# Key-value sums with the exponentiated keys stationary, and key projections in 128-column matmuls

## The chip, the cores and the metric

The kernel runs on one core of a Trainium2 chip. The metric is the device time of one execution in microseconds (us). TensorE (PE in the profile) multiplies matrices: a weight load (PEld) brings the stationary operand into the array, then a matmul streams the moving operand past it and writes to a bank of PSUM. VectorE (DVE), ScalarE (ACT) and GpSimd (POOL) do the rest; SyncE (SP) issues transfers.

## The reference

Linear attention with exponential features, then a feed-forward layer on its output:

```python
def phi(x):
    proj = np.einsum('bhsd,df->bhsf', x, w_phi)
    proj = proj - np.max(np.abs(proj), axis=-1, keepdims=True)
    return np.concatenate([np.exp(proj), np.exp(-proj)], axis=-1)
q_p, k_p = (phi(q), phi(k))
kv = np.einsum('bhsf,bhsd->bhfd', k_p, v)
z = np.sum(k_p, axis=2)
num = np.einsum('bhsf,bhfd->bhsd', q_p, kv)
den = np.einsum('bhsf,bhf->bhs', q_p, z)[..., None] + 1e-06
...
h = x @ w_in
g = np.maximum(0.01 * h, h)
return (g @ w_out).astype(np.float32)
```

There are 8 batches, 8 heads, 576 tokens, head size 64, 128 projected features (256 after the two exponentials); x has 4608 rows of 512, the hidden layer 2048. All is float32.

## The kernel before

**Precision.** A float32 matmul takes several passes, so most operands are split: a value rounded to the type F32R (names ending in h) and the remainder, again F32R (ending in l). A product is then the sum of three F32R matmuls, h with h, l with h and h with l, accumulated in one PSUM bank.

**Feed-forward.** 18 blocks of 256 tokens, each with 16 feature tiles. `layer1` (L549) issues 12 matmuls of 256 columns into a tile `h`; ScalarE and VectorE apply the leaky maximum (L559, L560), ScalarE rounds it to `gh`, POOL makes `gl`; `layer2` (L565), three tiles later, issues six matmuls of 512 columns into `acc`. Before a block, `split` (L537) rounds its rows of attention output (`xh`, `xl`).

**Attention.** A phase handles two heads of one batch: `k_phase(i)` and `q_phase(i)`, i from 0 to 31. The first four are written apart, for the start. Phases 4 to 7 of `k_phase` (`nat`) use float32 matmuls for the sums; phases 8 to 31, 24 of them, split. In such a phase each of the five 128-token chunks (the last has 64 tokens) is projected by two matmuls with the keys stationary (`ks`, in whose 128 rows rounded key and remainder of one head lie together) and 256 moving columns, `wq`, rounded weights beside their remainders (L231). The two halves of the result are added by ScalarE and VectorE (L235, L236). Then come the maximum (L239), the subtraction (L244) and two exponentials (L249, L250). Rounding gives `kph` and `kpl`. The sums then have the values stationary, `vh` (64 rounded values and two columns of ones) or `vl` (64 remainders), and 256 feature columns of keys moving, six matmuls for a chunk. For the last chunk rounded keys and remainders are stacked in 128 rows (`kst`), and `vl` multiplies 64 of them. All accumulate in one tile `c`, with features along the columns. ScalarE copies it (L275), four transposes turn it (L281), and it is rounded and split into `kvh` and `kvl` (L291 to L294), which `q_phase` uses as stationary operands (L358 to L363).

**Order.** The code emits instructions with priorities (attention ahead of the feed-forward layers), and a scheduler writes one fixed order for each engine. `advance` (L586) lets attention run ahead, up to two phases and the room in `ring`. Tiles are drawn from pools: `PBUFS` (L34) gives the eight PSUM banks to tags: three for `a` (projections and numerators), one for `c`, two for `h`, two for `acc`. A tile waits until the last reader of its buffer is done.

Of the kernel before, what the change touches and what calls it, by code (L numbers as in the profile page):

```python
# [9 lines left out]
F32 = mybir.dt.float32  # L10
F32R = mybir.dt.float32r
# [3 lines left out]
ALU = mybir.AluOpType  # L15
AX = mybir.AxisListType

P = 128
B, H, S, D = 8, 8, 576, 64
NP = H // 2  # L20
F = 128
# [8 lines left out]
LAG = 3  # L30
NN = 8
NK = 8
BUFS = {"kph": 2, "eq": 2, "m4": 2, "g": 2, "gh": 2, "gl": 2, "qh": 2, "ql": 2}
PBUFS = {"a": 3, "c": 1, "h": 2, "acc": 2}  # L34
ENG = {"vh": "a", "kst": "v", "qh": "v", "o": "av", "kl": "pv", "kpl": "pppv", "ksub": "vvp"}
TINY = 2.0 ** -15
HUGE = 2.0 ** 16 * 1.875
# [7 lines left out]
def attention_moe_kernel(ctx: ExitStack, tc: tile.TileContext, q, k, v, vt, w_phi, w_in, w_out, out):  # L45
    nc = tc.nc
# [16 lines left out]

    def copy_(key, o, i):
        e = pick(key) or "a"
        if e == "a":
            nc.scalar.copy(o, i)  # L67
        else:
            (nc.vector if e == "v" else nc.gpsimd).tensor_copy(o, i)  # L69

    def tt_(key, o, a, b, op):
        (nc.vector if pick(key) == "v" else nc.gpsimd).tensor_tensor(o, a, b, op=op)  # L72
# [23 lines left out]
    vh = ct([P, 10, 66], F32R, "vh")  # L96
    vl = ct([P, 10, 64], F32R, "vl")
    nc.gpsimd.memset(vh[:, :, 64:66].bitcast(F32), 1.0)
# [41 lines left out]
    for j in range(2):  # L140
        r = slice(64 * j, 64 * j + 64)
        c = slice(F * j, F * j + F)
# [46 lines left out]
    def k_phase(i):  # L189
        nat = i < NK  # L190
        rk, rv = kraw.pop(i)
        ks = st([P, 2, S], F32R, "ks")
        kh, kl = ks[:, 0], ks[:, 1]
        if nat:
            copy_("kh", kh, rk)
            tt_("kl", kl, rk, kh.bitcast(F32), ALU.subtract)
        else:
            for j in range(2):
                o, n = slice(64 * j, 64 * j + 64), slice(64 - 64 * j, 128 - 64 * j)
                copy_("kh", ks[o, j], rk[o])  # L200
                nc.vector.tensor_tensor(ks[n, j], rk[o], ks[o, j].bitcast(F32), op=ALU.subtract)
            copy_("vh", vh[:, :, 0:64], rv[:, :, 0:64])
            for r, c in ((slice(0, P), slice(0, 8)), (slice(64, P), slice(8, 10))):
                tt_("vl", vl[r, c], rv[r, c, 0:64], vh[r, c, 0:64].bitcast(F32), ALU.subtract)
        if i + 1 < B * NP:
            load_k(i + 1)
        yield
        kvp = pt("c")

        def kv_mm(j, lt, rt, first=False, last=False):  # L210
            nc.tensor.matmul(kvp[0 : lt.shape[1], 256 * j : 256 * j + 256], lhsT=lt, rhs=rt,  # L211
                             start=first and j == 0, stop=last, skip_group_check=True)

        for g in range(3):
            w = 2 if g < 2 else 1
            r = slice(0, P) if g < 2 else slice(64, P)
            n = P if g < 2 else 64
            m4 = st([P, 4], F32, "m4")
            pmk = st([P, 4, F], F32, "pmk")
            if nat:  # L220
                pk = pt("a")
                for s in range(w):
                    t0 = (2 * g + s) * P if g < 2 else S - P
                    proj(pk, s, kh[:, t0 : t0 + P], kl[:, t0 : t0 + P])
                pkv = pk[r, 0 : 256 * w].rearrange("p (a f) -> p a f", f=F)
            else:
                for s in range(w):
                    t0 = (2 * g + s) * P if g < 2 else S - P
                    pk = pt("a")
                    for j in range(2):  # L230
                        nc.tensor.matmul(pk[:, 256 * j : 256 * j + 256], lhsT=ks[:, j, t0 : t0 + P],  # L231
                                         rhs=wq.rearrange("p a f -> p (a f)"), start=True, stop=True)
                    pk = pk[r].rearrange("p (j x f) -> p j x f", j=2, x=2)
                    x = pmk[r, 2 * s : 2 * s + 2]
                    copy_("pk", x, pk[:, :, 1])  # L235
                    nc.vector.tensor_tensor(x, pk[:, :, 0], x, op=ALU.add)  # L236
                    yield
                pkv = pmk[r, 0 : 2 * w]
            nc.vector.tensor_reduce(m4[r, 0 : 2 * w], pkv, axis=AX.X, op=ALU.max, apply_absolute_value=True)  # L239
            mb = m4[r, 0 : 2 * w].unsqueeze(2).broadcast_to([n, 2 * w, F])  # L240
            if nat:
                nc.vector.tensor_tensor(pmk[r, 0 : 2 * w], pkv, mb, op=ALU.subtract)
            else:
                tt_("ksub", pkv, pkv, mb, ALU.subtract)  # L244
            yield
            for s in range(w):
                c = 2 * g + s
                ek = st([P, 2, 256], F32, ("ek", "kph", "kpl")[c % 3] if nat else "ek")
                nc.scalar.activation(ek[r, :, 0:F], pmk[r, 2 * s : 2 * s + 2], AF.Exp)  # L249
                nc.scalar.activation(ek[r, :, F:256], pmk[r, 2 * s : 2 * s + 2], AF.Exp, scale=-1.0)  # L250
                if nat:
                    for j in range(2):
                        kv_mm(j, rv[r, 4 * j + c if c < 4 else 8 + j], ek[r, j], first=c == 0, last=c == 4)
# [20 lines left out]
        kvs = st([P, 2, 256], F32, "ek").rearrange("p a (b f) -> p a b f", b=2)[0:66]  # L274
        copy_("kvs", kvs, kvp[0:66].rearrange("p (a b f) -> p a b f", a=2, b=2))  # L275
        yield
        kvt = pt("c")
        kvtv = kvt[:, 0:264].rearrange("p (a b f) -> p a b f", a=2, b=2)
        for j in range(2):
            for t in range(2):  # L280
                nc.tensor.transpose(kvtv[:, j, t], kvs[:, j, t], ident[0:66, 0:66])  # L281
        if i < NN:
            kvh = st([P, 2, 2, P], F32, "kvh")
            nc.scalar.copy(kvh[:, :, :, 0:64], kvtv[:, :, :, 0:64])
            nc.scalar.copy(kvh[:, :, :, 64:P], kvtv[:, :, :, 64:65].broadcast_to([P, 2, 2, 64]))
            kvs_of[i] = kvh, None
        else:
            kvh = st([P, 2, 2, P], F32R, "kvh")
            kvl = st([P, 2, 2, P], F32R, "kvl")
            zb = kvtv[:, :, :, 64:65].broadcast_to([P, 2, 2, 64])  # L290
            copy_("kvh", kvh[:, :, :, 0:64], kvtv[:, :, :, 0:64])  # L291
            copy_("kvh", kvh[:, :, :, 64:P], zb)
            nc.vector.tensor_tensor(kvl[:, :, :, 0:64], kvtv[:, :, :, 0:64], kvh[:, :, :, 0:64].bitcast(F32), op=ALU.subtract)
            nc.vector.tensor_tensor(kvl[:, :, :, 64:P], zb, kvh[:, :, :, 64:P].bitcast(F32), op=ALU.subtract)  # L294
            kvs_of[i] = kvh, kvl
        yield

# [362 lines left out]
```

## Time and profile before

| | |
|---|---|
| runs (three) | 1284.26, 1285.53, 1285.65 us; median 1285.53 |
| profiled execution | span 1285.0 us from first to last instruction; its time outside the span is not given |
| TensorE busy, matmuls | 1199.9 us, 7564, each with a weight load |
| VectorE, ScalarE, GpSimd busy | 972.6, 775.9, 778.4 us |
| TensorE clock granted | 0.973 on average, 1.00 from 300 to 1110 us |

A row of the timeline gives start and length in us, engine, line, operation, tiles written and read, and shapes; `x4` at its end merges four equal neighbours, and brackets show idle time before it and what ended it. A row of the groups gives the count, total busy us and mean ns of one, then the idle time before and its releasers. The length of a matmul row includes its latency; matmuls overlap, so their pace is read from start to start. In shapes, `128*66` is rows and columns of the stationary operand, `128x256` the moving one; the type reads f32 for F32R operands too.

### The profile page before, as it was taken

The page shows a single profiled execution, that of the slowest core. Times are in us where ns is not written, and L with a number is a line of the kernel's source. Part 1 is how long each engine was busy: PE and PEld are TensorE (multiplying, and loading weights), DVE is VectorE, ACT ScalarE, POOL GpSimd, SP SyncE. Part 2 cuts the span into 40 slices and gives each one's busy share as a digit, 9 for nine tenths or more (in the row PEclk, how much of TensorE's full clock was granted, in tenths as well). Part 3 has the DMA queues.
Part 4 walks back from the last instruction along what each step waited for, and adds up shares of the span by engine and source line. Part 5 has one row for each costly group of instructions (what it writes and reads, how often), then busy time and mean ns, then how long its engine had stood idle before and what let it go on. Part 6 is the DMA issues. An engine that isn't in the chain of part 4 may idle for free. (4 is left out here: it accounts for less than half of the span.)

```text
span 1285.0 us, 21831 instructions
## 1 busy us (share of the span) xinstructions
PE 1199.9 (93%) x7564; PEld 1045.4 (81%) x7564; DVE 972.6 (76%) x1685; ACT 775.9 (60%) x2014; POOL 778.4 (61%) x784
## 2 busy tenths in 40 slices
PE   7778879989999999999999999999999999999998
PEld 5457648868888888879888888989888988899997
DVE  7999996578898988888988998872888798611111
ACT  5454447666666776766767766753767766533232
POOL 3677754255676777676867677764677766533232
PEclk9789879999999999999999999999999999999999
DMA  7333341111110111111111111110111110000000
GB/s 202 113 88 97 118 121 46 40 35 29 30 43 24 46 30 46 30 37 38 29 46 30 45 30 37 30 36 11 36 30 46 30 37 1 17 18 1 18 17 17
DMA packets 62782, 57.05 MB, mean 44 GB/s; under 512 B 45136, under 2 KB 46288, under 8 KB 62672
## 3 DMA queue, kind: packets, MB, share of 16 engines
q1 hardware_dynamic: 62672, 55.65, 15.3%
q8 instruction: 60, 0.98, 0.3%
q14 instruction: 50, 0.41, 0.1%
HBM read 46.20 MB, written 9.44 MB: 43 GB/s over the span
## 5 line engine op out<-in xcount | busy, mean ns | idle before, releaser
L72 POOL TENSOR_TENSOR gl<-g,gh 128x256 fp32r<-128x256 f32 x288 | 241.5, 842 | 252.9 <-ACT gh L67 212.3
L552 PE MATMUL h<-xh,w0h 128*128 128x256 f32 x1152 | 300.1, 287 | 16.5 <-DVE g L560 14.8
L553 PE MATMUL h<-xh,w0l 128*128 128x256 f32 x1152 | 297.0, 285 | 0.4 <-POOL w0l L72 0.4
L560 DVE TENSOR_TENSOR g<-h,g 128x256 f32<-128x256 f32 x288 | 117.7, 413 | 177.3 <-ACT g L559 174.9
L552 PEld LDWEIGHTS h<-xh,w0h 128*128 128x128 f32 x1152 | 219.6, 191 | 32.4 <-DVE g L560 21.7
L573 PE MATMUL acc<-w1h,gh 128*128 128x512 f32 x576 | 229.2, 399 | 6.4 <-ACT gh L67 5.3
L574 PE MATMUL acc<-w1l,gh 128*128 128x512 f32 x576 | 228.3, 397 | 0.0
L553 PEld LDWEIGHTS h<-xh,w0l 128*128 128x128 f32 x1152 | 219.9, 191 | 8.2 <-POOL w0l L72 0.9
L575 PE MATMUL acc<-w1h,gl 128*128 128x512 f32 x576 | 217.6, 400 | 1.0 <-POOL gl L72 0.5
L555 PE MATMUL h<-xl,w0h 128*128 128x256 f32 x1152 | 203.4, 284 | 0.0
L72 POOL TENSOR_TENSOR ql<-eq,qh 128x576 fp32r<-128x576 f32 x96 | 161.3, 1687 | 52.4 <-DVE qh L69 47.8
L67 ACT CAST gh<-g 128x256 fp32r<-128x256 f32 x288 | 115.0, 403 | 125.4 <-PE acc L574 64.8
L559 ACT ACTIVATE g<-h 128x256 f32<-128x256 f32 x288 | 108.7, 382 | 109.4 <-PE h L555 80.4
L555 PEld LDWEIGHTS h<-xl,w0h 128*128 128x128 f32 x1152 | 166.4, 191 | 2.0 <-POOL xl L72 0.4
L573 PEld LDWEIGHTS acc<-w1h,gh 128*128 128x128 f32 x576 | 108.9, 189 | 23.2 <-ACT gh L67 5.9
L72 POOL TENSOR_TENSOR kpl<-ek,kph 128x512 fp32r<-128x512 f32 x72 | 104.4, 1450 | 30.8 <-ACT kph L67 18.9
L574 PEld LDWEIGHTS acc<-w1l,gh 128*128 128x128 f32 x576 | 108.9, 189 | 15.9
L575 PEld LDWEIGHTS acc<-w1h,gl 128*128 128x128 f32 x576 | 105.3, 190 | 18.9 <-POOL gl L72 1.6
L69 DVE CAST qh<-eq 128x576 fp32r<-128x576 f32 x96 | 82.6, 868 | 22.8 <-ACT eq L344 8.7
L343 ACT ACTIVATE eq<-mb 128x288 f32<-128x288 f32 x112 | 49.2, 439 | 69.9 <-DVE mb L338 58.8
L249 ACT ACTIVATE ek<-pmk 128x256 f32<-128x256 f32 (+1 forms) x128 | 53.3, 416 | 51.3 <-POOL pmk L72 21.4
L72 POOL TENSOR_TENSOR ring<-ring,mb 128x576 f32<-128x576 f32 (+2 forms) x40 | 50.6, 1265 | 47.1 <-DVE mb L372 37.2
(201 smaller groups left out, 2600.8 us busy)
## 6 DMA issues: line engine op xcount, KB each, us to landing
out_dram<-o SPq DMA_DIRECT2D x35, 256.0 KB, 2.0
rk<-in_k_dram SPq DMA_DIRECT2D x30, 288.0 KB, 2.8
ring<-in_w_in_dram SPq DMA_DIRECT2D x16, 512.0 KB, 3.6
ring<-in_w_out_dram SPq DMA_DIRECT2D x16, 512.0 KB, 3.6
rq<-in_q_dram SPq DMA_DIRECT2D x28, 288.0 KB, 2.8
rv<-in_v_dram SPq DMA_DIRECT2D x30, 256.0 KB, 3.5
rv<-in_vt_dram SPq DMA_DIRECT2D x60, 32.0 KB, 3.0
f<-in_k_dram SPq DMA_DIRECT2D x2, 288.0 KB, 3.9
```

Of the source, the lines that this page charges most:

```text
L67: nc.scalar.copy(o, i)
L69: (nc.vector if e == "v" else nc.gpsimd).tensor_copy(o, i)
L72: (nc.vector if pick(key) == "v" else nc.gpsimd).tensor_tensor(o, a, b, op=op)
L249: nc.scalar.activation(ek[r, :, 0:F], pmk[r, 2 * s : 2 * s + 2], AF.Exp)
L552: nc.tensor.matmul(ph, lhsT=weight(0, "h", ft)[:, d * P : d * P + P], rhs=xh[:, d], start=d == 0, stop=False)
L553: nc.tensor.matmul(ph, lhsT=weight(0, "l", ft)[:, d * P : d * P + P], rhs=xh[:, d], start=False, stop=False)
L555: nc.tensor.matmul(ph, lhsT=weight(0, "h", ft)[:, d * P : d * P + P], rhs=xl[:, d], start=False, stop=d == NP - 1)
L559: nc.scalar.mul(g, ph, 0.01)
L560: nc.vector.tensor_tensor(g, ph, g, op=ALU.max)
L573: nc.tensor.matmul(a, lhsT=gh[:, ts], rhs=weight(1, "h", ft), start=ft == 0, stop=False)
L574: nc.tensor.matmul(a, lhsT=gh[:, ts], rhs=weight(1, "l", ft), start=False, stop=False)
L575: nc.tensor.matmul(a, lhsT=gl[:, ts], rhs=weight(1, "h", ft), start=False, stop=ft == NFT - 1)
```

## The change

In the 24 split phases, the keys become stationary and the values moving. `va` holds for each chunk [64 rounded values, 2 ones, 64 remainders] = 130 columns (`VW`). A matmul takes 128 features of `kph` as stationary operand and all 130 columns, or of `kpl` and the first 66, so the sums come out with features along the partitions: two halves t for each head j, each head in its own tile `c`. The sums of the remainder columns stand apart (columns 66 to 130) and are added when `kvl` is made. Copy and transposes go; the roundings are made for each head, and the ones' part of `kvl` by a broadcast copy. The key projection now accumulates rounded weights and remainders in PSUM, two matmuls of 128 columns in place of one of 256, two chunks to a tile `a`; the halves' addition goes, and the subtraction of the maximum, always on VectorE, reads PSUM. The pool gives two buffers to `a` and two to `c`. The diff, without the deletion of code that it replaces one to one:

```diff
-PBUFS = {"a": 3, "c": 1, "h": 2, "acc": 2}
+VW = 130
+PBUFS = {"a": 2, "c": 2, "h": 2, "acc": 2}
...
-            for r, c in ((slice(0, P), slice(0, 8)), (slice(64, P), slice(8, 10))):
-                tt_("vl", vl[r, c], rv[r, c, 0:64], vh[r, c, 0:64].bitcast(F32), ALU.subtract)
+            copy_("vh", va[:, :, 0:64], rv[:, :, 0:64])
+            tt_("vl", va[:, :, 66:VW], rv[:, :, 0:64], va[:, :, 0:64].bitcast(F32), ALU.subtract)
...
+        kvps = [pt("c")] if nat else [pt("c"), pt("c")]
...
+        def kv_mm(j, x, v, first=False, last=False):
+            for t in range(2):
+                nc.tensor.matmul(kvps[j][:, VW * t : VW * t + v.shape[1]], lhsT=x[:, t * F : t * F + F], rhs=v,
+                                 start=first and t == 0, stop=last, skip_group_check=True)
...
-                    for j in range(2):
-                        nc.tensor.matmul(pk[:, 256 * j : 256 * j + 256], lhsT=ks[:, j, t0 : t0 + P],
-                                         rhs=wq.rearrange("p a f -> p (a f)"), start=True, stop=True)
-                    copy_("pk", x, pk[:, :, 1])
-                    nc.vector.tensor_tensor(x, pk[:, :, 0], x, op=ALU.add)
+                for j in range(2):
+                    o = pk[:, (2 * s + j) * F : (2 * s + j) * F + F]
+                    nc.tensor.matmul(o, lhsT=ks[:, j, t0 : t0 + P], rhs=wq_h, start=True, stop=False)
+                    nc.tensor.matmul(o, lhsT=ks[:, j, t0 : t0 + P], rhs=wq_l, start=False, stop=True)
...
-                tt_("ksub", pkv, pkv, mb, ALU.subtract)
+            nc.vector.tensor_tensor(pmk[r, 0 : 2 * w], pkv, mb, op=ALU.subtract)
...
-                        kv_mm(j, vh[:, 4 * j + c], kph[:, j], first=c == 0)
-                        kv_mm(j, vl[:, 4 * j + c], kph[:, j])
+                        kv_mm(j, kph[:, j], va[:, 4 * j + c], first=c == 0)
...
-                        kv_mm(j, vh[:, 4 * j + c], kpl[:, j])
+                        kv_mm(j, kpl[:, j], va[:, 4 * j + c, 0:66])
...
-                        kv_mm(j, vl[r, 8 + j], kst[r, j])
-                        kv_mm(j, vh[:, 8 + j], kst[:, j], last=True)
+                        kv_mm(j, kst[:, j], va[:, 8 + j], last=True)
...
-            zb = kvtv[:, :, :, 64:65].broadcast_to([P, 2, 2, 64])
-            copy_("kvh", kvh[:, :, :, 0:64], kvtv[:, :, :, 0:64])
-            copy_("kvh", kvh[:, :, :, 64:P], zb)
-            nc.vector.tensor_tensor(kvl[:, :, :, 0:64], kvtv[:, :, :, 0:64], kvh[:, :, :, 0:64].bitcast(F32), op=ALU.subtract)
-            nc.vector.tensor_tensor(kvl[:, :, :, 64:P], zb, kvh[:, :, :, 64:P].bitcast(F32), op=ALU.subtract)
+            d = st([P, 2, 2, 66], F32, "ek")
+            for j in range(2):
+                kv = kvps[j][:, 0 : 2 * VW].rearrange("p (t c) -> p t c", t=2)
+                copy_("kvh", kvh[:, j, :, 0:64], kv[:, :, 0:64])
+                copy_("kvh", kvh[:, j, :, 64:P], kv[:, :, 64:65].broadcast_to([P, 2, 64]))
+                nc.vector.tensor_tensor(d[:, j], kv[:, :, 0:66], kvh[:, j, :, 0:66].bitcast(F32), op=ALU.subtract)
+                nc.vector.tensor_tensor(kvl[:, j, :, 0:64], kv[:, :, 66:VW], d[:, j, :, 0:64], op=ALU.add)
+            copy_("kvh", kvl[:, :, :, 64:P], d[:, :, :, 64:65].broadcast_to([P, 2, 2, 64]))
```

The scheduler's order moves with it. First TensorE's order around one chunk of key-value sums, before block 4 (a name ending in `_1112` or the like is a buffer number; the new code's lines 546, 547, 567, 568 and 569 are the old 552, 553, 573, 574 and 575, and 215 is the key-value matmul, 232 and 233 the key projection). Before:

```order
L552 MATMUL h<-xh,w0h_1112 128x256
L211 MATMUL c<-kph,vh 66x256
L211 MATMUL c<-kph,vl 64x256
L211 MATMUL c<-kph,vh 66x256
L211 MATMUL c<-kph,vl 64x256
L553 MATMUL h<-xh,w0l_1113 128x256
L552 MATMUL h<-xh,w0h_1112 128x256
L553 MATMUL h<-xh,w0l_1113 128x256
L231 MATMUL a<-wq,ks 128x256 x2
L319 MATMUL a<-qs,wq 128x288
L320 MATMUL a<-qs,wq 128x288
L211 MATMUL c<-kpl,vh 66x256 x2
```

and now:

```order
L568 MATMUL acc<-w1l_1033,gh 128x512
L215 MATMUL c<-va,kph 128x130 x4
L569 MATMUL acc<-w1h_1032,gl 128x512
L567 MATMUL acc<-w1h_1032,gh 128x512
L568 MATMUL acc<-w1l_1033,gh 128x512
L569 MATMUL acc<-w1h_1032,gl 128x512
L546 MATMUL h<-xh,w0h_1111 128x256
L547 MATMUL h<-xh,w0l_1112 128x256
L546 MATMUL h<-xh,w0h_1111 128x256
L215 MATMUL c<-va,kpl 128x66 x4
```

A chunk is eight narrow matmuls in two groups of four, where it was four and two wide ones; the projection's pairs become groups of four. In all the program's MATMULs rise by 336.

The second place is TensorE's order where layer 1 of block 4 begins, the first block that reads the third batch of attention. Before:

```order
L574 MATMUL acc<-w1l_1126,gh 128x512
L552 MATMUL h<-xh,w0h_836 128x256
L553 MATMUL h<-xh,w0l_837 128x256
L555 MATMUL h<-xl,w0h_836 128x256
L281 MATMUL c<-ident,ek 128x66 x4
L231 MATMUL a<-wq,ks 128x256 x2
L555 MATMUL h<-xl,w0h_836 128x256
```

and now, from the last numerators of the third batch on (in the cut: the key projections, 288-column query projections and one group of key-value matmuls of later phases):

```order
L357 MATMUL a<-ql,kvh 128x288 x2
L232 MATMUL a<-wq,ks 128x128
L233 MATMUL a<-wq,ks 128x128
...
L313 MATMUL a<-qs,wq 128x288
L314 MATMUL a<-qs,wq 128x288
L215 MATMUL c<-va,kph 128x130 x4
L232 MATMUL a<-wq,ks 128x128
...
L546 MATMUL h<-xh,w0h_835 128x256
L547 MATMUL h<-xh,w0l_836 128x256
L549 MATMUL h<-xl,w0h_835 128x256 x3
```

Before, the numerators of that batch stand some 45 layer matmuls earlier, and layer matmuls run on with only small attention groups between. Now 20 key matmuls and eight query projections of later phases, and no layer matmul, stand between the last numerators and layer 1. The same rows recur at block 6; at block 2 both orders have such a place.

More of the change, by code (lines that the diff above doesn't have):

```diff
@@ L95, in attention_moe_kernel @@
     bd_h, bd_l = bd[:, 0], bd[:, 1]
-    vh = ct([P, 10, 66], F32R, "vh")
-    vl = ct([P, 10, 64], F32R, "vl")
-    nc.gpsimd.memset(vh[:, :, 64:66].bitcast(F32), 1.0)
+    va = ct([P, 10, VW], F32R, "va")
+    nc.gpsimd.memset(va[:, :, 64:66].bitcast(F32), 1.0)
     fr1, fr4 = (cp.tile([P, 2048], F32R, tag="late", name=n, bufs=4) for n in ("fr1", "fr4"))
@@ L201, in k_phase @@
                 nc.vector.tensor_tensor(ks[n, j], rk[o], ks[o, j].bitcast(F32), op=ALU.subtract)
-            copy_("vh", vh[:, :, 0:64], rv[:, :, 0:64])
-            for r, c in ((slice(0, P), slice(0, 8)), (slice(64, P), slice(8, 10))):
-                tt_("vl", vl[r, c], rv[r, c, 0:64], vh[r, c, 0:64].bitcast(F32), ALU.subtract)
+            copy_("vh", va[:, :, 0:64], rv[:, :, 0:64])
+            tt_("vl", va[:, :, 66:VW], rv[:, :, 0:64], va[:, :, 0:64].bitcast(F32), ALU.subtract)
         if i + 1 < B * NP:
@@ L207, in k_phase, with kv_nat @@
         yield
-        kvp = pt("c")
-        def kv_mm(j, lt, rt, first=False, last=False):
-            nc.tensor.matmul(kvp[0 : lt.shape[1], 256 * j : 256 * j + 256], lhsT=lt, rhs=rt,
+        kvps = [pt("c")] if nat else [pt("c"), pt("c")]
+        def kv_nat(j, lt, rt, first=False, last=False):
+            nc.tensor.matmul(kvps[0][0 : lt.shape[1], 256 * j : 256 * j + 256], lhsT=lt, rhs=rt,
                              start=first and j == 0, stop=last, skip_group_check=True)
+        def kv_mm(j, x, v, first=False, last=False):
+            for t in range(2):
+                nc.tensor.matmul(kvps[j][:, VW * t : VW * t + v.shape[1]], lhsT=x[:, t * F : t * F + F], rhs=v,
+                                 start=first and t == 0, stop=last, skip_group_check=True)
         for g in range(3):
@@ L219, in k_phase @@
             pmk = st([P, 4, F], F32, "pmk")
[L220 to L223, printed above, removed]
+            pk = pt("a")
+            for s in range(w):
+                t0 = (2 * g + s) * P if g < 2 else S - P
+                if nat:
                     proj(pk, s, kh[:, t0 : t0 + P], kl[:, t0 : t0 + P])
[L225 to L229, printed above, removed]
-                    for j in range(2):
-                        nc.tensor.matmul(pk[:, 256 * j : 256 * j + 256], lhsT=ks[:, j, t0 : t0 + P],
-                                         rhs=wq.rearrange("p a f -> p (a f)"), start=True, stop=True)
-                    pk = pk[r].rearrange("p (j x f) -> p j x f", j=2, x=2)
-                    x = pmk[r, 2 * s : 2 * s + 2]
-                    copy_("pk", x, pk[:, :, 1])
-                    nc.vector.tensor_tensor(x, pk[:, :, 0], x, op=ALU.add)
-                    yield
-                pkv = pmk[r, 0 : 2 * w]
+                    continue
+                for j in range(2):
+                    o = pk[:, (2 * s + j) * F : (2 * s + j) * F + F]
+                    nc.tensor.matmul(o, lhsT=ks[:, j, t0 : t0 + P], rhs=wq_h, start=True, stop=False)
+                    nc.tensor.matmul(o, lhsT=ks[:, j, t0 : t0 + P], rhs=wq_l, start=False, stop=True)
+            pkv = pk[r, 0 : 256 * w].rearrange("p (a f) -> p a f", f=F)
             nc.vector.tensor_reduce(m4[r, 0 : 2 * w], pkv, axis=AX.X, op=ALU.max, apply_absolute_value=True)
             mb = m4[r, 0 : 2 * w].unsqueeze(2).broadcast_to([n, 2 * w, F])
-            if nat:
-                nc.vector.tensor_tensor(pmk[r, 0 : 2 * w], pkv, mb, op=ALU.subtract)
-            else:
-                tt_("ksub", pkv, pkv, mb, ALU.subtract)
+            nc.vector.tensor_tensor(pmk[r, 0 : 2 * w], pkv, mb, op=ALU.subtract)
             yield
@@ L252, in k_phase @@
                     for j in range(2):
-                        kv_mm(j, rv[r, 4 * j + c if c < 4 else 8 + j], ek[r, j], first=c == 0, last=c == 4)
+                        kv_nat(j, rv[r, 4 * j + c if c < 4 else 8 + j], ek[r, j], first=c == 0, last=c == 4)
                     yield
@@ L270, in k_phase @@
                     for j in range(2):
-                        kv_mm(j, vl[r, 8 + j], kst[r, j])
-                        kv_mm(j, vh[:, 8 + j], kst[:, j], last=True)
+                        kv_mm(j, kst[:, j], va[:, 8 + j], last=True)
                 yield
[L274 to L282, printed above, removed]
+        if nat:
+            kvs = st([P, 2, 256], F32, "ek").rearrange("p a (b f) -> p a b f", b=2)[0:66]
+            copy_("kvs", kvs, kvps[0][0:66].rearrange("p (a b f) -> p a b f", a=2, b=2))
+            yield
+            kvt = pt("c")
+            kvtv = kvt[:, 0:264].rearrange("p (a b f) -> p a b f", a=2, b=2)
+            for j in range(2):
+                for t in range(2):
+                    nc.tensor.transpose(kvtv[:, j, t], kvs[:, j, t], ident[0:66, 0:66])
             kvh = st([P, 2, 2, P], F32, "kvh")
@@ L289, in k_phase @@
             kvl = st([P, 2, 2, P], F32R, "kvl")
-            zb = kvtv[:, :, :, 64:65].broadcast_to([P, 2, 2, 64])
-            copy_("kvh", kvh[:, :, :, 0:64], kvtv[:, :, :, 0:64])
-            copy_("kvh", kvh[:, :, :, 64:P], zb)
-            nc.vector.tensor_tensor(kvl[:, :, :, 0:64], kvtv[:, :, :, 0:64], kvh[:, :, :, 0:64].bitcast(F32), op=ALU.subtract)
-            nc.vector.tensor_tensor(kvl[:, :, :, 64:P], zb, kvh[:, :, :, 64:P].bitcast(F32), op=ALU.subtract)
+            d = st([P, 2, 2, 66], F32, "ek")
+            for j in range(2):
+                kv = kvps[j][:, 0 : 2 * VW].rearrange("p (t c) -> p t c", t=2)
[4 more added lines that the diff above has]
+            copy_("kvh", kvl[:, :, :, 64:P], d[:, :, :, 64:65].broadcast_to([P, 2, 2, 64]))
             kvs_of[i] = kvh, kvl
```

## The prediction

> **What bounds the kernel now.** I read the page's busy times first, then the same by stretches, then matmuls one by one. The page's line on TensorE, and three stretches (each engine's busy time with its instruction count, then granted clock, DMA share, GB/s):
>
> ```profile
> PE 1199.9 (93%) x7564; PEld 1045.4 (81%) x7564; DVE 972.6 (76%) x1685; ACT 775.9 (60%) x2014; POOL 778.4 (61%) x784
> 0.00:150.00 150.00, 114.63 (x579) 89.30 (x580) 140.57 (x237) 73.43 (x187) 98.47 (x100) 0.86 0.43 123
> ...
> 277.90:295.40 17.50, 11.13 (x50) 7.51 (x48) 14.45 (x25) 10.62 (x27) 3.33 (x4) 0.80 0.11 35
> ...
> 300.00:1110.00 810.00, 784.75 (x5185) 698.23 (x5184) 682.02 (x1169) 555.88 (x1447) 552.84 (x530) 1.00 0.12 33
> ```
>
> Every matmul has a weight load of its own (7564 of each). From 300 to 1110 us, where 23 of the 24 changed key phases run, TensorE is busy 785 of 810 us at full clock, VectorE 682. What TensorE issues there is paid in time, unless it stood idle; so I need the pace of its instructions, start to start, since a row's length includes pipeline latency. TensorE rows (start us, length us), first the wide matmuls of layer 2, then the key-value sums as they are:
>
> ```profile
> 600.33 0.39 PE L575 MATMUL acc<-w1h,gl 128*128 128x512 f32 x1
> 600.56 0.39 PE L573 MATMUL acc<-w1h,gh 128*128 128x512 f32 x1
> ...
> 602.19 0.28 PE L211 MATMUL c<-kph,vh 128*66 128x256 f32 x1
> ...
> 602.66 0.28 PE L552 MATMUL h<-xh,w0h 128*128 128x256 f32 x1
> ...
> 603.01 0.29 PE L553 MATMUL h<-xh,w0l 128*128 128x256 f32 x1
> ```
>
> 512 moving columns take 0.23 us; four matmuls of 256 columns (602.19 to 602.66) take 0.47, 0.1175 each: 0.46 ns a column and hardly a fixed cost. Layer 1, with 128 stationary columns, keeps the same pace (602.66 to 603.01 is three of them), so a 128-column weight load hides under 256 moving columns. Whether it hides under 128 is the question. The nearest place is the start-up query unit of 64 tokens, where four narrow matmuls with 128 stationary columns stand together. The weight loads there:
>
> ```profile
> 117.50 0.53 PEld L500 LDWEIGHTS c<-eq,qh 128*128 128x128 f32 x4
> 117.95 0.19 PEld L379 LDWEIGHTS a<-bd,ks 128*128 128x128 f32 x1
> 118.06 0.19 PEld L380 LDWEIGHTS a<-bd,ks 128*128 128x128 f32 x1
> ```
>
> Five loads start between 117.50 and 118.06: 0.11 us each. The matmuls stream only 64 columns (0.06 us or less), yet their loads follow each other at 0.112. A single load appears to be prefetched, and loads do not overlap each other. These are float32 operands and not the rounded kind; but a 128-column load of the rounded kind has the same length:
>
> ```profile
> L552 PEld LDWEIGHTS h<-xh,w0h 128*128 128x128 f32 x1152 | 219.6, 191 | 32.4 <-DVE g L560 21.7 <-ACT xh L67 1.9 <-ACT g L559 0.9
> L211 PEld LDWEIGHTS c<-kph,vl 128*64 128x64 f32 x192 | 25.8, 134 | 3.5
> ```
>
> The 64-column load is 57 ns shorter, 0.9 ns a column, which again makes a 128-column load about 0.114 us.
>
> **The change on TensorE.** Counts of what it replaces:
>
> ```profile
> L211 PE MATMUL c<-kph,vh 128*66 128x256 f32 x240 | 64.5, 287 | 2.6 <-DVE kvl L294 1.6 <-ACT kph L67 0.9
> L231 PE MATMUL a<-wq,ks 128*128 128x256 f32 x240 | 49.6, 288 | 0.1
> L211 PE MATMUL c<-kph,vl 128*64 128x256 f32 x192 | 49.4, 280 | 0.0
> L211 PE MATMUL c<-kpl,vh 128*66 128x256 f32 x192 | 38.9, 284 | 1.0 <-DVE kpl L72 0.5 <-POOL kpl L72 0.4
> L211 PE MATMUL c<-kph,vl 64*64 64x256 f32 x48 | 16.0, 334 | 1.1 <-DVE kph L69 1.1
> L281 PE MATMUL c<-ident,ek 66*128 66x66 f32 x112 | 11.9, 228 | 0.0
> ```
>
> and three places of the timeline: four transposes, and a key-value matmul over 64 rows between its neighbours.
>
> ```profile
> 359.28 0.41 PE L281 MATMUL c<-ident,ek 66*128 66x66 f32 x4
> 359.50 0.48 PE L555 MATMUL h<-xl,w0h 128*128 128x256 f32 x2
> ...
> 623.71 0.28 PE L553 MATMUL h<-xh,w0l 128*128 128x256 f32 x1
> 623.91 0.33 PE L211 MATMUL c<-kph,vl 64*64 64x256 f32 x1
> 624.17 0.51 PE L231 MATMUL a<-wq,ks 128*128 128x256 f32 x2
> ```
>
> A changed phase (of 24) has 10 projection and 28 key-value matmuls. 36 of them are of the plain kind: 36 x 0.1175 = 4.23 us. The two with 64 rows are dearer: the neighbour before waits 0.20 instead of 0.1175 (623.71 to 623.91), its own pace is 0.26; 0.35 us each, 0.70 together. Four transposes take 0.22 (359.28 to 359.50). Together 5.15 us.
>
> Afterwards there are 20 projection matmuls of 128 columns and 36 key-value matmuls of 130 or 66 columns, 56 in all, each with 128 stationary columns, none with 64 rows, no transposes. The streamed columns fall from 9,728 to 6,216, but the loads rise from 38, many of them short, to 56 full ones. At 0.1125 a load: 6.30 us. That is +1.15 us a phase, +27.6 us for 24. I take 0.1125 because the start-up rows are nearest: narrow moving operand, 128 stationary columns. At 0.105 it would be +17.5.
>
> **Order and PSUM.** Two tiles tagged a instead of three, two c instead of one. The price of a block boundary at which layer 1 waits for attention can be read today at the one where this happens (layer 1 of block 2):
>
> ```profile
> 280.56 1.24 PE L358 MATMUL a<-eq,kvh 128*128 128x288 f32 x4 [2.02 <-ACT eq L343]
> 281.73 0.51 PE L231 MATMUL a<-wq,ks 128*128 128x256 f32 x2
> ...
> 285.68 0.40 PE L319 MATMUL a<-qs,wq 128*128 128x288 f32 x1 [1.31 <-DVE tq L321]
> 286.79 0.61 PE L319 MATMUL a<-qs,wq 128*128 128x288 f32 x1 [0.57 <-DVE tq L321]
> 288.21 0.47 PE L211 MATMUL c<-kph,vl 64*64 64x256 f32 x1 [0.56 <-DVE kph L69]
> 289.97 0.41 PE L552 MATMUL h<-xh,w0h 128*128 128x256 f32 x1
> ```
>
> In the 17.5 us from 277.9 to 295.4 TensorE ran 50 matmuls, about 6.3 us at the paces above: 11 us lost to waits and to the clock, granted at 0.80 there. In the new order layer 1 waits in this way at blocks 4 and 6 too (the second pair of excerpts above): attention work stands alone behind the last query matmuls, and its a-tiles (each read by ScalarE or VectorE before reuse) have two buffers. Bounds: 0 where the fillers cover the chain, 11 each as today. The fillers at block 4 are 20 narrow and 8 wide matmuls, some 3.3 us, against a chain of two ScalarE copies, two transposes and a reciprocal on VectorE, POOL's multiplication (1.47 us, row below) and a rounding, estimated at 5 us by the rows of such operations here, and on top of it the waits of nine fillers for two a-buffers. I take 5 each, near the middle: +10. In the start-up, where the pool of a is used too, fewer buffers are costed at nothing: VectorE, busy 141 of the first 150 us, covers it; without that cover they would cost a few microseconds.
>
> **The other engines.** Rows of what goes or shrinks:
>
> ```profile
> L67 ACT COPY pmk<-a 128x256 f32<-128x256 f32 x96 | 33.1, 372 | 5.9 <-PE a L231 5.1
> L236 DVE TENSOR_TENSOR pmk<-a,pmk 128x256 f32<-128x256 f32 x96 | 36.6, 399 | 1.7 <-ACT pmk L67 1.3
> L72 DVE TENSOR_TENSOR pmk<-pmk,m 128x512 f32<-128x512 f32 x48 | 45.8, 955 | 0.5
> L242 DVE TENSOR_TENSOR pmk<-a,m 128x512 f32<-128x512 f32 x8 | 5.4, 678 | 0.1
> L72 POOL TENSOR_TENSOR pmk<-pmk,m 64x256 f32<-64x256 f32 x24 | 15.5, 645 | 27.5 <-DVE m L239 19.0 <-PE a L320 4.2 <-PE a L231 2.7
> L72 POOL TENSOR_TENSOR ring<-ring,mb 128x576 f32<-128x576 f32 x28 | 41.1, 1466 | 43.5 <-DVE mb L372 37.2 <-PE a L320 3.5 <-ACT pmk L67 1.9
> L67 ACT COPY ek<-c 66x512 f32<-66x512 f32 x28 | 16.3, 583 | 16.1 <-PE c L211 14.7 <-DVE g L560 1.3
> PE h L552 <- DVE g L560: 11.6, 16, 1.8
> PE a L358 <- DVE qh L69: 6.3, 9, 1.5
> ```
>
> ScalarE loses five copies (1.9 us a phase) and the 0.58 copy of the sums, and gains some 0.8 in smaller roundings and one broadcast copy: -1.6. VectorE loses five adds (2.0), saves 0.13 on the subtraction (two of 0.955 become 0.678 each, but it takes over POOL's of the third group, estimated 0.43), and gains four small operations for two (estimated +0.4): -1.75. POOL loses that subtraction, 0.65, and has one value remainder to make instead of two. No DMA is added or moved past another. All this is off TensorE's path; it pays only by shortening TensorE's waits, whose largest kinds from 300 to 1110 us are the last two rows (us in total, times, longest), 18 us; the smaller kinds add 7. VectorE's load falls by 1.75 in 28 us a phase (682 over 24). I take -8, between 0 and -25 (all of those waits). The new chain at a phase's end (roundings and subtractions straight from PSUM instead of copy, transposes, roundings, subtractions) is shorter; I cost it at nothing, covered by layer matmuls.
>
> Sum against the profiled span: 1285.0 + 27.6 + 10 - 8 = 1314.6. The runs' median is 1285.5, half a microsecond above the span, so 1315.
>
> **Rivals.**
> - *Narrow matmuls run at their streamed pace (faster).* The transposes speak for it: 128-column loads, yet 0.055 us apart. Then 20 x 0.059 + 20 x 0.060 + 16 x 0.055 = 3.25 us a phase, -1.90, -45.6 in all: 1285.5 - 45.6 + 2 = 1242. Against it: those loads are shorter (L281 loads are of the transposing kind), and the rows at 117.50 are plain ones. It decides once a narrow pair costs less than 5.15 / 56 = 0.092 us. The Trainium skill (TensorE: Matmul & The Clock Gate, Back-to-back issue gap) puts a stream of load-and-matmul pairs at about 81 ns for 128 columns and 131 for 512: by it 56 x 0.081 = 4.54 us, -15 in all, 1273. The trace does not agree on 512 columns (230 ns), and its narrow pairs stand at 112.
> - *Narrow rounded matmuls are streamed several times over (much slower).* No rounded matmul here has under 256 columns. Unrounded ones show what a fallback costs: the two matmuls of 288 columns at 280.56 have four records and the next starts at 281.73, so 0.58 us a matmul (0.05 of it the first load) against 0.13 at the rounded pace, four times as much. Then 20 x 0.235 + 20 x 0.239 + 16 x 0.121 = 11.4 us a phase, +150: 1438. Against it: the program has one matmul and one load for each of them, as for the wide ones.
> - *The relief pays for the loads (no change, or slightly faster).* With loads at 0.105, boundaries at nothing and all 25 us of waits gone: 1285.5 + 17.5 - 25 = 1278; half of that gives 1284. Against it: the waits on L560 are on a chain of four operations, not on VectorE's load alone.
>
> **Chances.** Loads bind, 1315: 0.68 (its own range 1293 to 1335, from loads at 0.105 to 0.1125, boundaries 0 to 11 each, relief 0 to -25). Streamed pace, 1242: 0.14. Relief pays, about 1284: 0.08. Several passes, 1438: 0.10. A measurement tells 0.2%, 2.6 us, from no change. Faster: 0.14, half of the third case, a tail: 0.19. Same: 0.04. Slower: 0.77. The range takes in the likeliest case and reaches down to the middle of the streamed one, 1242 to 1340; it leaves out the several-pass case and half of the streamed one.
>
> **What would show it.** Right: loads of the 128x130 and 128x66 matmuls start 0.11 us apart, TensorE's busy share rises while VectorE and ScalarE fall by some 40 us each, and waits of several microseconds stand before layer 1 of blocks 4 and 6. Wrong: narrow matmuls 0.06 us apart (the sum turns negative), or over 0.2 (several passes).

## The result, and the profile after

| | before | after |
|---|---|---|
| median of four runs | 1284.89 us | 1340.74 us |
| ratio, 95% interval | | 1.0431, 1.0416 to 1.0446 |
| profiled span | 1285.0 us | 1336.4 us |
| granted TensorE clock, mean | 0.973 | 0.955 |

The change makes the kernel 4.3% slower. The prediction had the sign and most of the mechanism, but its 1315 is short by 26 us, and the time lies 0.7 us above the range. Times of experiments are medians; one execution each of experiments 1, 4 and 5, which took 2916, 6462 and 1699 us, is left out, and since it is the profiled one in 1 and 4, the traces of these two are read for the order of instructions alone. The page's busy times after:

```profile
PE 1236.1 (92%) x7900; PEld 1108.9 (83%) x7900; DVE 900.4 (67%) x1637; ACT 749.2 (56%) x1942; POOL 717.1 (54%) x736
```

TensorE has 336 more matmuls and loads; VectorE lost 72 us of work, ScalarE 27, POOL 61, where the prediction had some 40 for each of the first two; and TensorE's busy share did not rise, it fell from 93 to 92%. The loads of a projection group in the changed kernel (start us, length us):

```profile
603.85 0.19 PEld L232 LDWEIGHTS a<-wq,ks 128*128 128x128 f32 x1
603.96 0.19 PEld L233 LDWEIGHTS a<-wq,ks 128*128 128x128 f32 x1
604.07 0.19 PEld L232 LDWEIGHTS a<-wq,ks 128*128 128x128 f32 x1
604.18 0.19 PEld L233 LDWEIGHTS a<-wq,ks 128*128 128x128 f32 x1
```

They start 0.11 us apart, as foretold from the start-up rows of before. Now the place where layer 1 of block 4 waits. It does not begin there: twelve of its matmuls, on the first three quarters of `xh`, stand from 434.0 us on, and it waits for the last quarter. TensorE's rows (idle before and its releaser in brackets):

```profile
443.61 0.53 PE L357 MATMUL a<-ql,kvh 128*128 128x288 f32 x2 [0.32 <-POOL ql L73]
...
445.85 0.40 PE L313 MATMUL a<-qs,wq 128*128 128x288 f32 x1 [0.86 <-ACT tq L360]
446.09 0.29 PE L314 MATMUL a<-qs,wq 128*128 128x288 f32 x1
448.27 0.58 PE L313 MATMUL a<-qs,wq 128*128 128x288 f32 x1 [1.89 <-DVE pmk L237]
...
450.63 0.41 PE L232 MATMUL a<-wq,ks 128*128 128x128 f32 x1
450.84 0.41 PE L233 MATMUL a<-wq,ks 128*128 128x128 f32 x1
...
452.92 0.41 PE L546 MATMUL h<-xh,w0h 128*128 128x256 f32 x1
453.13 0.41 PE L547 MATMUL h<-xh,w0l 128*128 128x256 f32 x1
```

After the last numerators (L357) no layer matmul comes for 9 us. The query projections (L313) wait for an a-tile that ScalarE (L360) or VectorE (L237) still has to read: the two buffers. Then the pace itself drops to little over half: narrow pairs 0.21 us apart instead of 0.11, 256-column ones 0.21 instead of 0.118. The clock was granted at half from 446.7 to 456.9 us. So an idle place is paid twice, by the wait and by what follows at half clock.

To compare kernels I split each profiled span. "Work" is the count of matmuls times the undisturbed pace of their kind (256 columns 0.118 us, 288 0.133, 512 0.232, narrow 0.1115, transposes 0.061, unrounded ones 0.216 for each record of 256 columns, two to a matmul); "lost" is the rest of the start-to-start time: waits, half clock, and the stalls round 64-row matmuls. The two sum to the span less some 10 us at its ends.

| kernel | work | lost |
|---|---|---|
| before | 1123.0 | 151.6 |
| after | 1159.4 | 166.7 |

Of the lost time before, 48 x 0.23 = 11 us are the 64-row stalls. By blocks, from one block's first layer-1 matmul to the next's, the loss is 17.3, 4.5, 6.6 and 4.7 us in blocks 2, 4, 6 and 13 before, and 24.0, 14.2, 14.2 and 15.5 after. The other blocks from 3 on lose 25 us less than before, 15 against 40; up to block 2 it is 83.7 us after against 78.9.

### The profile page after: what moved, and what is told of

Read it like the earlier page. It is cut to its first block, busy times and chain, and to the rows that moved or that the text cites. A ratio compares the mean times of both kernels' runs of the same rounds, so it can differ in the third digit from the quotient of the medians.

```text
span 1336.4 us, 22258 instructions
## 1 busy us (share of the span) xinstructions
PE 1236.1 (92%) x7900; PEld 1108.9 (83%) x7900; DVE 900.4 (67%) x1637; ACT 749.2 (56%) x1942; POOL 717.1 (54%) x736
## 3 DMA queue, kind: packets, MB, share of 16 engines
q1 hardware_dynamic: 62672, 55.65, 14.8%
## 5 line engine op out<-in xcount | busy, mean ns | idle before, releaser
L73 POOL TENSOR_TENSOR gl<-g,gh 128x256 fp32r<-128x256 f32 x288 | 230.0, 802 | 307.6 <-ACT gh L68 262.9
L569 PE MATMUL acc<-w1h,gl 128*128 128x512 f32 x576 | 220.7, 400 | 0.5 <-POOL gl L73 0.5
L73 POOL TENSOR_TENSOR ql<-eq,qh 128x576 fp32r<-128x576 f32 x96 | 143.2, 1500 | 72.5 <-DVE qh L70 46.1
L549 PEld LDWEIGHTS h<-xl,w0h 128*128 128x128 f32 x1152 | 169.2, 195 | 1.5 <-POOL xl L73 0.6
L73 POOL TENSOR_TENSOR kpl<-ek,kph 128x512 fp32r<-128x512 f32 x72 | 96.2, 1336 | 97.9 <-PE c L215 36.8
L215 PEld LDWEIGHTS c<-va,kph 128*128 128x128 f32 x480 | 70.5, 201 | 22.0 <-DVE kph L261 12.8
L70 DVE CAST qh<-eq 128x576 fp32r<-128x576 f32 x96 | 75.0, 802 | 18.7 <-ACT eq L338 8.0
L215 PE MATMUL c<-va,kph 128*128 128x130 f32 x480 | 73.8, 279 | 14.5 <-DVE kph L261 10.4
```

The costliest lines, as they stand in the source:

```text
L215: nc.tensor.matmul(kvps[j][:, VW * t : VW * t + v.shape[1]], lhsT=x[:, t * F : t * F + F], rhs=v, start=first and t == 0, stop=last, skip_ ...
L549: nc.tensor.matmul(ph, lhsT=weight(0, "h", ft)[:, d * P : d * P + P], rhs=xl[:, d], start=False, stop=d == NP - 1)
L569: nc.tensor.matmul(a, lhsT=gl[:, ts], rhs=weight(1, "h", ft), start=False, stop=ft == NFT - 1)
```

## The experiments

Ratios are against the kernel before, run beside each. All experiments keep the rest of their kernel; but the scheduler plans the whole order anew for each.

**1. The new pool in the kernel before.**

```diff
-PBUFS = {"a": 3, "c": 1, "h": 2, "acc": 2}
+PBUFS = {"a": 2, "c": 2, "h": 2, "acc": 2}
```

> The kernel before with only the PSUM pool of the changed kernel: two buffers for tag a and two for c. PSUM theory: the boundary stalls come from the pool. The new order puts the last numerators behind the last layer matmul at blocks 4, 6, 13 and 15, as in the changed kernel; each such boundary loses some 10 us, so 1315 to 1330 us. Rival, narrow groups: attention is late because the narrow matmuls take longer; then the pool alone costs nothing and this runs at 1285 to 1290.

1326.75 us, ratio 1.0319 (1.0302 to 1.0337). With not one matmul changed the pool costs 41 us. Its order has at most four layer matmuls between the last numerators of a batch and the first remainder matmul (L555) of blocks 4, 6, 13 and 15, where the kernel before has 46, 52, 148 and 155. The pool theory holds, the rival that narrow groups delay attention falls. (In the changed kernel block 15 is no such place: 41 layer matmuls stand between, and it loses 1.4 us.)

**2. The changed kernel with three buffers for a.**

```diff
-VW = 130
-PBUFS = {"a": 2, "c": 2, "h": 2, "acc": 2}
+VW = 128
+PBUFS = {"a": 3, "c": 1, "h": 2, "acc": 2}
...
-        kvps = [pt("c")] if nat else [pt("c"), pt("c")]
+        kvps = [pt("c")]
```

> The changed kernel with three buffers for a and one for c. To fit both heads in one bank it leaves out the two columns of ones, so a moving operand has 128 or 64 columns and the denominators are replaced by another sum; the number of matmuls and loads is the same. PSUM theory: the boundary stalls at blocks 4, 6 and 13 go (about 40 us in the changed kernel against 16 before) and the relief of VectorE and ScalarE stays: 1285 + 25 for the loads - 15 = 1295, at most 1305. Narrow groups: 1330 to 1342, as the changed kernel.

1319.16 us, ratio 1.0263 (1.0248 to 1.0278): 21.6 us less than the changed kernel, but 14 more than I allowed. Work 1159.4, lost 147.3. The stalls at blocks 4, 6 and 13 are gone and block 2 is as before: these four lose 7.2, 4.7, 3.3 and 17.6 us. The first 24 us of block 4, by the view of stretches, in the changed kernel, in this one and in the kernel before:

```profile
434.00:458.00 24.00, 19.54 (x109) 17.73 (x107) 17.96 (x31) 14.83 (x39) 15.70 (x14) 0.79 0.14 39
```

```profile
439.90:463.90 24.00, 23.76 (x166) 21.67 (x166) 15.28 (x31) 16.23 (x47) 16.46 (x18) 1.00 0.12 37
```

```profile
423.90:447.90 24.00, 22.99 (x153) 20.22 (x153) 21.92 (x41) 16.88 (x46) 20.28 (x23) 1.00 0.17 50
```

The first pair in brackets is TensorE's matmuls: 109 in the changed kernel at clock 0.79, 166 with the third buffer at full clock. Little is left of the relief: the kernel before without 64-row matmuls (experiment 6) lost 150.7 us, this one 147.3.

**3. The projection alone.**

```diff
-                    for j in range(2):
-                        nc.tensor.matmul(pk[:, 256 * j : 256 * j + 256], lhsT=ks[:, j, t0 : t0 + P],
-                                         rhs=wq.rearrange("p a f -> p (a f)"), start=True, stop=True)
...
-                    copy_("pk", x, pk[:, :, 1])
-                    nc.vector.tensor_tensor(x, pk[:, :, 0], x, op=ALU.add)
+                for j in range(2):
+                    o = pk[:, (2 * s + j) * F : (2 * s + j) * F + F]
+                    nc.tensor.matmul(o, lhsT=ks[:, j, t0 : t0 + P], rhs=wq_h, start=True, stop=False)
+                    nc.tensor.matmul(o, lhsT=ks[:, j, t0 : t0 + P], rhs=wq_l, start=False, stop=True)
```

> The kernel before, its pool and its key-value sums, with only the new key projection (20 matmuls of 128 columns for 10 of 256, no copies and adds). Loads theory: all of the load cost is here, 24 x (20 x 0.1115 - 10 x 0.1175) = +25 us of TensorE work, less some relief of VectorE and ScalarE: 1295 to 1310. If narrow pairs cost in proportion to their share of the new loads (20 of 56) it would be +9: 1285 to 1294.

1302.37 us, ratio 1.0123 (1.0108 to 1.0138). Work 1148.2, +25.2 as expected; lost 141.2, 10 less. Here the relief is there.

**4. The key-value sums alone, new pool.** The reverse of 3, applied to the changed kernel.

> The changed kernel with the old key projection: new key-value sums and the new pool (a 2, c 2). Loads theory: 36 narrow matmuls at 0.1115 (4.01 us a phase) replace 26 of 0.1175, two over 64 rows (0.35 each) and four transposes (4.0 in all), so TensorE's work equals that of the kernel before; what is left is the pool's cost, 1310 to 1325, nearly that of the kernel before with the new pool. If the 36 narrow matmuls themselves cost, work is 15 us above it and the time 1325 to 1340.

1298.59 us, ratio 1.0103 (1.0086 to 1.0120): below both forecasts, and 28 us below experiment 1 with the same pool and projection. Under the small pool the new sums help; with three buffers (experiment 7) they do not. One part can be read from the order: here 68 layer matmuls stand between the last numerators and the first remainder matmul of block 13, in experiment 1 four. By the loss of block 13 in experiment 8 against before, 12.8 against 4.7, that is some 8 of the 28 us, an estimate. The rest is not settled.

**5. Wider moving operands, as many loads.**

```diff
+WW = 208
...
-                        kv_mm(j, kph[:, j], va[:, 4 * j + c], first=c == 0)
+                        kv_mm(j, kph[:, j], vf[:, VW * (4 * j + c) : VW * (4 * j + c) + WW], first=c == 0)
```

and likewise for `kpl` and `kst`; `vf` is `va` with its chunks in a row.

> The changed kernel with every moving operand of the key-value sums 208 columns wide instead of 130 or 66 (the columns behind belong to the next chunk and are not read; the second key remainder meets the value remainders too). Loads and matmuls are as many as before. Loads theory: 208 columns stream in about 0.096 us, still under the 0.111 of a load, so nothing is added: 1335 to 1350, with the pace of these matmuls unchanged at 0.111. Streamed-columns rival: 0.096 against 0.060 and 0.030, 1.6 us a phase, some +38 us: 1378.

1335.53 us, ratio 1.0379 (1.0362 to 1.0396): no slower than the changed kernel, though these matmuls stream 208 columns for 130 or 66. Four of them between two rows:

```profile
617.48 0.59 PE L218 MATMUL c<-va,kph 128*128 128x208 f32 x4
617.91 0.31 PE L355 MATMUL a<-qh,kvh 128*128 128x288 f32 x1
```

0.43 us for four, 0.11 each. The load sets the pace; the streamed columns under it are free. A fixed cost of every matmul would look the same, but the float32 transposes speak against it: they move 66 columns at 0.061 us each, and their loads, 66 rows by 128 columns, are shorter (142 ns against 190).

**6. No 64-row matmuls in the kernel before.**

```diff
-            for r, c in ((slice(0, P), slice(0, 8)), (slice(64, P), slice(8, 10))):
-                tt_("vl", vl[r, c], rv[r, c, 0:64], vh[r, c, 0:64].bitcast(F32), ALU.subtract)
+            tt_("vl", vl[:, :, :], rv[:, :, 0:64], vh[:, :, 0:64].bitcast(F32), ALU.subtract)
...
-                        kv_mm(j, vl[r, 8 + j], kst[r, j])
+                        kv_mm(j, vl[:, 8 + j], kst[:, j])
```

> The kernel before with the value remainders of the last chunk in all 128 rows, so that no key-value matmul has 64 rows; the remainders of the keys then meet the value remainders too. Theory that those two matmuls a phase cost 0.35 us each instead of 0.1175: -0.23 us x 48 = -11 us, 1273 to 1278. Rival, the stall falls into time in which TensorE would have waited anyway: 1283 to 1287.

1285.78 us, ratio 0.9990 (0.9980 to 0.9999). The stalls are gone, the 11 us are not gained: lost time is 150.7 against 151.6. Waits of this kernel (us in total, times, longest), to be held against the two rows of before, 11.6 and 6.3:

```profile
PE h L551 <- DVE g L559: 14.7, 15, 3.0
PE a L357 <- DVE qh L69: 8.0, 10, 1.6
```

Both grew, by 5 us together: that much of the TensorE time saved became waiting on VectorE's chain. The other 6 us are spread over smaller gaps, and no single wait shows them.

**7. The key-value sums alone, three buffers.** As 2, with the projection of before.

> The new key-value sums with the old key projection and three buffers for a, one for c; to fit one bank it leaves out the columns of ones, as in the run with three buffers above. TensorE's work should equal the kernel before (36 x 0.1115 against 26 x 0.1175 + 0.70 + 0.22 a phase). If the key-value part costs nothing beyond work: 1280 to 1290. If it brings waits of its own (the run with three buffers stood 17 us above the run with the projection alone): 1297 to 1307.

1306.65 us, ratio 1.0152 (1.0137 to 1.0167): the second case. Work 1134.2, 11 above the kernel before; the 11 us of 64-row stalls that should pay for it are worth nothing (experiment 6). Lost 158.9, another 8 above experiment 6. The largest wait, of layer 1 on VectorE's leaky maximum, is 19.2 us from 300 to 1130, 14.7 in experiment 6.

**8. Two buffers for a, one for c, in the kernel before.** `PBUFS = {"a": 2, "c": 1, ...}`, one bank unused.

> The kernel before with two buffers for a and one for c (one bank unused). If the third buffer of a is what keeps the boundaries apart: as with two and two, 1320 to 1335, and the trace shows 10 us lost at blocks 4, 6, 13 and 15 each. If the second c is what hurts: 1285 to 1290.

1320.11 us, ratio 1.0258 (1.0241 to 1.0276). The third a-buffer alone is worth 33 us. Blocks 2, 4, 6, 13 and 15 lose 19.9, 14.2, 14.8, 12.8 and 12.2 us; work is 1123.0 as before. Its first 24 us of block 4:

```profile
423.50:447.50 24.00, 19.35 (x94) 14.57 (x93) 21.48 (x32) 16.40 (x40) 16.17 (x15) 0.85 0.11 35
```

94 matmuls at clock 0.85 against 153 at 1.00: the picture of the changed kernel, with the old matmuls.

**9. A wide projection without copies and adds.** On experiment 6:

```diff
-            for j in range(2):
-                o, n = slice(64 * j, 64 * j + 64), slice(64 - 64 * j, 128 - 64 * j)
-                copy_("kh", ks[o, j], rk[o])
-                nc.vector.tensor_tensor(ks[n, j], rk[o], ks[o, j].bitcast(F32), op=ALU.subtract)
+        copy_("kh", kh, rk)
+        tt_("kl", kl, rk, kh.bitcast(F32), ALU.subtract)
...
+            pk = pt("a")
+            for s in range(w):
+                t0 = (2 * g + s) * P if g < 2 else S - P
+                proj(pk, s, kh[:, t0 : t0 + P], kl[:, t0 : t0 + P])
```

`proj` issues three matmuls of 256 columns against a block-diagonal weight; copies and adds go as in 3.

> A candidate. The kernel before with no 64-row matmul and with the key projection of phases 4 to 7 in all phases: both heads' rounded keys against a block-diagonal weight of 256 columns, three wide matmuls a chunk (15 a phase) instead of two wide (10) or four narrow (20); keys are rounded in one operation and split in one, instead of two and two. It has the relief of the new projection (no copies and adds, the maximum taken from PSUM) without its narrow loads. TensorE's work: +5 x 0.1175 x 24 = +14 us. If relief on VectorE and ScalarE pays as in the run with the projection alone (-10), and the cheaper split of the keys (VectorE about 2.3 us a phase less) as much again: 1272 to 1285. If TensorE's work alone counts: 1299.

1287.35 us, ratio 1.0004 (0.9995 to 1.0013), between the two cases, a miss. Work 1137.1 (+14.1), lost 137.6 (-13). The largest wait now:

```profile
PE c L205 <- DVE kph L246: 14.0, 16, 1.6
```

**10. The same with the 64-row matmuls.**

> The same with the 64-row matmuls left in. If TensorE's waits absorb what the 64-row matmuls cost, as in the run that removed them alone, both run alike (within 3 us). If with VectorE relieved TensorE is the bound, this one is 8 to 11 us slower.

1290.73 us, ratio 1.0029 (1.0018 to 1.0041): 3.4 us above 9, between the two cases; neither is shown.

**11. The last chunk's rounding on ScalarE, on top of 9.**

```diff
-ENG = {"vh": "a", "kst": "v", ...}
+ENG = {"vh": "a", "kst": "a", ...}
```

> The candidate before (wide block-diagonal projection, no 64-row matmul), with the rounding of the last chunk's keys on ScalarE instead of VectorE. In the candidate TensorE waited 14 us, 16 times, for the stacked last chunk, made by two VectorE operations in a row. If that wait is VectorE's queue, most of it goes: 1274 to 1282. If another wait takes its place, 1284 to 1290.

1269.61 us, ratio 0.9870 (0.9852 to 0.9887): 1.3% faster than the kernel before, and than the changed kernel by 5%; better than the first case allowed. Work 1137.1 as in 9, lost 120.3. The wait of 9, here:

```profile
PE c L205 <- DVE kph L246: 1.8, 4, 0.8
```

That wait gives 12 of the 17 us of lost time that went.

**12. That rounding on ScalarE, on top of 6.**

> The kernel before with no 64-row matmul and the rounding of the last chunk's keys on ScalarE; its projection, copies and adds stay. If the gain of the last run came from the last chunk's chain alone (its VectorE operation), and the 64-row matmuls' 11 us now show: 1270 to 1278. If the wide projection's relief is needed: 1282 to 1288.

1292.24 us, ratio 1.0044 (1.0030 to 1.0058): slower than 6 by 6 us, outside both cases. Lost 155.9. So the engine of the rounding is no gain by itself; with the projection of 9 it is one of 18 us. Every small edit replans the order, and some 5 us either way follow that I can't put down to a mechanism.

## Why the prediction was wrong

Its three terms, in spans (1285.0 to 1336.4, +51.4):

| term | forecast | shown |
|---|---|---|
| loads on TensorE | +27.6 | +35.5: work +36.4; the 64-row stalls, forecast at -11.2, gave -0.9 (lost time, experiment 6 against before) |
| order and PSUM | +10 | +19.4: lost time, after against experiment 2 |
| relief of VectorE and ScalarE | -8 | -3.4: lost time, experiment 2 against 6 |

Of the 22 us that are missing, 8 are in the first term, 9 in the second and 5 in the third. Each figure compares two profiled executions whose order was planned anew, so some 5 us of it can be chance; and experiments 2 and 7 hold both heads' sums in one tile without the columns of ones, so they differ from the changed kernel by a little more than the pool.

**The pace of narrow matmuls** was right, 0.1115 us for the 0.1125 forecast. Of the rivals, the streamed pace and the several passes both fall: 0.11 us apart, and still 0.11 at 208 columns. The Trainium skill (TensorE: Matmul & The Clock Gate, LDWEIGHTS) has the load's time follow its columns, divided by 1.2, which is an estimate of 107 ns for 128; the rows with 128 rows and 128 columns agree within 5 ns, the loads of the transposes, 66 rows by 128 columns, do not (0.06 us apart). Its figure of 81 ns for a stream of 128-column pairs (Back-to-back issue gap) does not hold for these operands.

**The step that failed first is the one on order and PSUM**: "I take 5 each, near the middle: +10". The mechanism was named and the price of such a place was on the table, 11 us at block 2. The discount to 5 had no row to stand on: the chain of some 5 us and the fillers of 3.3 were weighed, while the waits of the fillers for two a-buffers were named and given no price, and half clock, which the 11 us held, was left out of the weighing. The upper bound was about right: blocks 4, 6 and 13 lost 14.2, 14.2 and 15.5 us where before lost 4.5, 6.6 and 4.7. And I counted two places where the order has three, block 13 with them. The order was there to be counted: between the last numerators of a batch and the first remainder matmul (L555) stand 46, 52 and 148 layer matmuls at blocks 4, 6 and 13 before, and 2, 2 and 4 after.

The start-up, put at nothing, cost too: up to block 2 the loss is 83.7 us after against 79.1 in experiment 2, and 85.0 in experiment 8 against 78.9 before. With these 5 us, blocks 2, 4, 6 and 13 lose 40 us more after than in experiment 2; the remaining blocks lose 20 less, 15 against 36. So the +19.4 of the table is a balance. That the forecast came within ten of it is partly luck: it had neither block 13 and the start-up nor what the other blocks give back, and what makes these lose less is not shown.

I also took the pool as one edit with a small price. Experiments 1 and 8 put its price, without any other change, at 41 and 33 us, of which 33 is the third buffer of a.

**The loads** were too cheap because the 64-row stalls were booked with them, 0.70 us a phase where plain matmuls take 0.235, as time that would be gained. Experiment 6 takes them away and gains 1 us. I had treated every microsecond of TensorE as paid in time; for what is taken away that does not hold in this kernel. For what is added the experiments can't tell: in 3 and 9 work rose by 25 and 14 us and the time by 16 and 1, but each also relieves VectorE and ScalarE.

**The relief** came, and somewhat larger than forecast: the new projection takes 10 us off the lost time (3 against before), or 12 (2 against 7). What the term left out are waits that the new key-value sums bring: they add 8 us of lost time (7 against 6), or 6 (2 against 3). The prediction has them only in its sentence on the new chain at a phase's end, "I cost it at nothing"; whether it is that chain is open.

**The range** ended at 1340 because the several-pass case was left out and the likeliest case ended at 1335; with boundaries at their own upper bound in three places and no relief, its own terms give 1285.5 + 27.6 + 33 = 1346. The lower end of the likeliest case, 1293, does not follow from its terms either: they give 1285.5 + 17.5 - 25 = 1278.

What stays open: why the new key-value sums save 28 us under two a-buffers (4 against 1) and cost 21 with three (7 against 6). The new projection differs as much: on top of the new sums it costs 42 us under two a-buffers (after against 4) and 13 with three (2 against 7). So the parts do not add up to the whole, and the projection alone under the new pool was not run.

## What to carry to other kernels

A matmul whose stationary operand is 128 rows by 128 columns of 4-byte values took the time of its load, 0.11 us here, whether 66, 128, 130 or 208 columns moved past it; at 0.46 ns a column, cutting moving columns below some 240 (an estimate from these two figures) saves nothing unless the number of loads falls too. A PSUM buffer taken from a pipeline that others wait for is not a detail: count in the new order how far ahead of each deadline its last result stands, and where it falls behind, take the price of such a place from the trace and do not discount it without a row. And time saved on the busiest engine need not shorten the kernel where a chain through another engine ends later (experiment 6): the fastest version here, experiment 11, adds matmuls to TensorE and takes operations out of VectorE's chain.

## What the hardware showed that I had not expected

A wait of a few microseconds cost more than itself: at block 4 TensorE's named waits are 3 us from 443 to 449, and from 446.7 us on the clock was granted at half for 10 us. Over the execution half clock lasted 120 us after the change against 72 before. Some 61 and 55 us of this lie in the first 200 us; after the change another 58 lie at blocks 2, 4, 6 and 13, while before has some 18 in all the rest. The mean clock fell from 0.973 to 0.955. The Trainium skill (TensorE: Matmul & The Clock Gate, The HAM clock gate) describes an array that halves its clock after an idle window; the trace agrees on the half, with 0.21 us for a pair that takes 0.11 at full clock, though the longest single wait around 446.7 us is 1.89 us.
